# Text rows on 64 neighbouring partitions, transposed by one DMA instead of nine matrix products

## The chip, the cores and the metric

The kernel runs on one core of a Trainium2 chip. A core has a matrix engine (TensorE, "PE" in the profile; "PEld" is its loading of weights), VectorE ("DVE"), ScalarE ("ACT"), GpSimd ("POOL") and SyncE ("SP"), which work through their own instruction lists in order and wait for one another by semaphores, and 16 DMA engines that all queues share. SyncE, ScalarE and GpSimd can issue transfers, each on a queue of its own. The metric is device time in microseconds, lower is better.

## The reference

It is the joint attention block of a diffusion transformer, for two batches of 256 image tokens and 32 text tokens with 1152 features, one attention head over all features, in bfloat16. Image and text have weights of their own. Cut to what matters:

```python
mod_t = (_silu(c) @ wmod_txt).reshape(B, 6, 1, D)      # the same for the image
sht, sct, gat = mod_t[:, 0], mod_t[:, 1], mod_t[:, 2]
hi = _layernorm(x_img) * (1 + sci) + shi
ht = _layernorm(x_txt) * (1 + sct) + sht
qkvi = hi @ wqkv_img
qkvt = ht @ wqkv_txt
q, k, v = concat text and image rows of each
p = softmax(q @ k^T * D ** -0.5)
a = p @ v
out_i = x_img + gai * (a_img @ wo_img)
out_t = x_txt + gat * (a_txt @ wo_txt)
```

The change concerns `ht`: the text of both batches, 64 rows, is normalised, brought to features on partitions, scaled by `1 + sct` and shifted by `sht`. TensorE then needs it as the operand of the text's q, k and v.

## The kernel before

The 1152 features are KT = 9 tiles of 128. All instructions are issued in an order written out by hand (a manual schedule); each engine's list is the program text's order, so what a function issues stands on each engine's list where the function is called.

The weights, some 39 MB, come by SyncE's queue in the order of use, each matrix as `[128, 9, 1152]` into one of five buffers of a pool (`load_w`, line 73; some go to a home of their own). A load waits until its buffer's last reader is done. Each transfer also takes one of eight completion counters in turn and waits until the transfer that had it before has landed.

Work on the image comes first: normalising, transposing, scaling, then v, then q (`qk_img(w_q_i, 0, ...)`, line 519). Meanwhile VectorE forms the shift's part of v (`shift_products`, lines 468 to 474) in `sacc`. Then comes the stretch around the change, the image's k (line 589):

`qk_img` (line 503) walks over the nine output tiles j of k: the first three together, then one each. Every one is nine products of 128x512 summed in PSUM (`qkps`, line 512) and is evicted to `kT` by ScalarE or VectorE, as the list K_ENG says (j = 2, 4, 5, 6, 7 by ScalarE; 3 and 8 by VectorE). Before tile j it calls `hooks[j]`, so other work is put between the tiles:

- before j=3 `txt_norm`: VectorE takes statistics of x_t, ScalarE the square root, VectorE writes the normalised text back to x_t (line 179); ScalarE also loads the table of the exponential.
- before j=6 `row_strips`: TensorE forms the text's shift and scale as rows (`tsh`, `tsc`, line 402), evicted by ScalarE and VectorE, and the strip `svr`, evicted by ScalarE. GpSimd sends svr through device memory to `v_t` (lines 535 and 539).
- before j=7 `cols_and_transposes`: small products turn these rows into columns (`select_cols`, lines 418 and 420, `ctp`), evicted to `mod_t` by VectorE (line 423) and ScalarE (line 426). Then `txt_transposes` (line 559) multiplies each 128-column tile of x_t with every second column of the identity, which transposes it and picks the 64 text rows in one (line 565, into `tpt` in PSUM). VectorE multiplies with the scale out of PSUM (line 566), in two pieces, and adds the shift (line 569) in two. The result is hT_t, `[128, 9, 64]`.
- before j=8 `qk_txt(w_q_t, 0)`: 81 products of 128x64 with hT_t make the text's q (line 580).

After j=8, `qk_txt(w_k_t, 1)` makes the text's k, and scores, softmax, the text's v and the gates, attention, and the output products follow.

Before the change x_t has 128 partitions: the 64 text rows are loaded to every second one (line 444), and a memset by GpSimd (line 123) has put zeros into the others, so that normalising can run over all 128. The scale's weights `w_sc_t` come by two transfers.

Of the kernel before, what the change touches and what calls it, by code (L numbers as in the profile page):

```python
# [14 lines left out]
def kernel(  # L15
# [14 lines left out]
    nc = tc.nc  # L30
    bf = mybir.dt.bfloat16
    f32 = mybir.dt.float32
    PSUM = bass.MemoryType.PSUM

    B, NI, D = x_img.shape
    NT = x_txt.shape[1]
    P = 128
    KT = D // P
# [3 lines left out]
    NTT = B * NT  # L42
# [13 lines left out]
    work = ctx.enter_context(tc.tile_pool(name="work", bufs=2))  # L56
    small = ctx.enter_context(tc.tile_pool(name="small", bufs=4))
    ps_mm = ctx.enter_context(tc.tile_pool(name="ps_mm", bufs=7, space=PSUM))
# [6 lines left out]
    xt_flat = x_txt.rearrange("b n d -> (b n) d")  # L65
# [4 lines left out]
    def w_view(src):  # L70
        return src.rearrange("(kt p) n -> p kt n", p=P)

    def load_w(src, c0, ksplits=((0, KT),), home=None):
        t = wpool.tile([P, KT, D], bf, tag="w", name="t") if home is None else act.tile([P, KT, D], bf, tag=home, name="w_home")
        for (k0, k1) in ksplits:
            nc.sync.dma_start(t[:, k0:k1, :], w_view(src)[:, k0:k1, c0:c0 + D])
        return t
# [5 lines left out]
    x_t = act.tile([P, D], bf)  # L83
# [30 lines left out]
    K2 = ((0, 5), (5, KT))  # L114
# [4 lines left out]
    ident = const.tile([P, P], bf)  # L119
    make_identity(nc, ident[:])  # L120
    eps_t = const.tile([P, 1], f32)
    nc.vector.memset(eps_t[:], EPS)
    nc.gpsimd.memset(x_t[:], 0.0)
    wz = const.tile([P, VW], bf)
    nc.vector.memset(wz[:], 0.0)  # L125
    sT32 = const.tile([P, KT, 32], bf)
# [35 lines left out]
    def ln_stats(x_ap, np_, k0=0, k1=NCH, stats=None):  # L162
        if stats is None:
            stats = small.tile([P, NCH, 6], f32, tag="stats")
        for k in range(k0, k1):
            nc.vector.bn_stats(stats[0:np_, k, :], x_ap[:, k * CH:(k + 1) * CH])  # L166
        return stats

    def ln_std(stats, np_):
        mv = small.tile([P, 2], f32, tag="mv")  # L170
        nc.vector.bn_aggr(mv[0:np_, :], stats[0:np_, :, :])
        rstd = small.tile([P, 1], f32, tag="rstd")
        nc.scalar.activation(rstd[0:np_, :], mv[0:np_, 1:2], ACT.Sqrt, bias=eps_t[0:np_, :])
        return mv, rstd

    def ln_apply(x_ap, np_, out_ap, mv, rstd, c0=0, c1=D):
        if c0 == 0:
            nc.vector.reciprocal(rstd[0:np_, :], rstd[0:np_, :])
        nc.vector.tensor_scalar(out_ap[:, c0:c1], x_ap[:, c0:c1], mv[0:np_, 0:1], rstd[0:np_, :],
                                op0=ALU.subtract, op1=ALU.mult)  # L180
# [107 lines left out]
    lns = {}  # L288
# [59 lines left out]
    k0, k1 = KC[2]  # L348
# [14 lines left out]
    k0 = KC[3][0]  # L363
# [76 lines left out]

    w_k_i = load_w(wqkv_img, D, K3)
    w_sh_t = load_w(wmod_txt, 0)
    w_sc_t = load_w(wmod_txt, D, K2)
    nc.sync.dma_start(x_t[0:P:P // NTT, :], xt_flat[:, :])
    w_q_t = load_w(wqkv_txt, 0, K2)
    w_k_t = load_w(wqkv_txt, D, K2)
    w_ga_i = load_w(wmod_img, 2 * D, K2, home="V")
# [12 lines left out]
    def qk_evac(out_ap, in_ap, blk, eng=None):  # L460
        if blk == 0:
            nc.scalar.mul(out_ap, in_ap, SCALE)  # L462
        else:
            evac(out_ap, in_ap, eng)
# [15 lines left out]
    def shift_low(b):  # L480
        if b == 0:
            lo = work.tile([P, D], bf, tag="o", bufs=3, name="slo")
        else:
            lo_full = act.tile([P, D + 32], bf, name="slo_full")
            lo = lo_full[:, 0:D]
        sparts[1, b] = lo
        nc.vector.tensor_sub(lo[:, 0:D], saccs[b][:], sparts[0, b][:])
# [15 lines left out]
    def qk_img(wq, blk, jg, hooks):  # L503

        groups = [(0, jg)] + [(j, j + 1) for j in range(jg, KT)]
        for (j0, j1) in groups:
            if j0 in hooks:
                hooks[j0]()
            pss = [ps_mm.tile([P, B * NI], f32, tag="mm", name="qkps") for _ in range(j0, j1)]
            for kt in range(KT):  # L510
                for j in range(j0, j1):
                    nc.tensor.matmul(pss[j - j0][:], lhsT=wq[:, kt, j * P:(j + 1) * P], rhs=hT_i[:, kt, :],  # L512
                                     start=(kt == 0), stop=(kt == KT - 1))
            for j in range(j0, j1):
                qk_evac(qkTs[blk][:, j, :, 0:NI], pss[j - j0][:].rearrange("p (b n) -> p b n", b=B), blk, K_ENG[j])
# [27 lines left out]
    sv = sv_full[:, 0:KT * B].rearrange("p (k b) -> p k b", b=B)  # L543
    hT_t = act.tile([P, KT, NTT], bf)
    def txt_norm():
        lns = ln_std(ln_stats(x_t[:, :], P), P)
        shift_low(1)
        ln_apply(x_t[:, :], P, x_t[:, :], *lns)
        junk = small.tile([P, 1], f32, bufs=1)
        nc.scalar.activation(junk[:], eps_t[:], ACT.Exp)  # L550

    def all_cols():
        ctps = (ps_mm.tile([P, NCOL + B], f32, tag="mm", name="ctp"), ps_sm.tile([P, NCOL + B], f32, tag="sm", name="ctp"))
        for ctp, rows in zip(ctps, (strips["tsh"], strips["tsc"])):
            select_cols(rows, ctp)
        cols_out(mod_t[:, 1, :, :], ctps[1], 1.0)
        cols_copy(mod_t[:, 0, :, :], ctps[0])

    def txt_transposes():
        pick = ident[:].rearrange("p (t r) -> p r t", r=P // NTT)[:, 0, :]  # L560
        hv = hT_t[:].rearrange("p k (b t) -> p k b t", b=B)
        for k0, k1 in ((0, 5), (5, KT)):
            tpt = ps_mm.tile([P, 5, NTT], f32, tag="mm")
            for kt in range(k0, k1):
                nc.tensor.matmul(tpt[:, kt - k0, :], lhsT=x_t[:, kt * P:(kt + 1) * P], rhs=pick, start=True, stop=True)
            nc.vector.tensor_mul(hv[:, k0:k1], tpt[:, 0:k1 - k0, :].rearrange("p k (b t) -> p k b t", b=B),
                                 mod_t[:, 1, k0:k1, :].unsqueeze(3).to_broadcast([P, k1 - k0, B, NT]))
        for k0, k1 in ((0, 5), (5, KT)):
            nc.vector.tensor_add(hv[:, k0:k1], hv[:, k0:k1],
                                 mod_t[:, 0, k0:k1, :].unsqueeze(3).to_broadcast([P, k1 - k0, B, NT]))  # L570
# [3 lines left out]
    def qk_txt(wq, blk):  # L574
        for j0 in range(0, KT, FG):
            jn = min(FG, KT - j0)
            ps = ps_mm.tile([P, FG, NTT], f32, tag="mm")
            for j in range(j0, j0 + jn):
                for kt in range(KT):
                    nc.tensor.matmul(ps[:, j - j0, :], lhsT=wq[:, kt, j * P:(j + 1) * P], rhs=hT_t[:, kt, :],  # L580
                                     start=(kt == 0), stop=(kt == KT - 1))
            qk_evac(qkTs[blk][:, j0:j0 + jn, :, NI:NTOK],
                    ps[:, 0:jn, :].rearrange("p j (b n) -> p j b n", b=B), blk)

    def cols_and_transposes():
        all_cols()
        txt_transposes()

    qk_img(w_k_i, 1, 3, hooks={3: txt_norm, 6: row_strips, 7: cols_and_transposes, 8: lambda: qk_txt(w_q_t, 0)})
    qk_txt(w_k_t, 1)  # L590


# [330 lines left out]
```

## Time and profile before

| | |
|---|---|
| time, median of 3 runs | 114.87 us (114.75 to 115.28) |
| the profiled execution: its own time | 115.62 us |
| the profiled execution: span | 113.8 us |
| TensorE busy | 109.1 us (96%) |
| VectorE busy | 76.0 us (67%) |
| ScalarE busy | 37.4 us (33%) |
| GpSimd busy | 27.6 us (24%) |
| moved by DMA | 40.87 MB, mean 359 GB/s |
| mean granted TensorE clock | 0.998 |

The span runs from the first to the last instruction of one profiled execution; the device time has some two microseconds around it. An engine's busy share alone does not say whether it sets the end: for that there is the chain that ended last, followed back from the last instruction through whatever released each step. A row of the profile gives the engine, the line of the kernel, the operation, what it writes and reads, how often, and in brackets the idle time ahead of it with what ended it. In the rows in order of time the first number is the start in microseconds from the span's start and the second the length. In the rows of transfers the numbers are the size of each in KB and the microseconds from issue to landing.

### The profile page before, as it was taken

Reading aid. Unit: us, or ns where it says so; the run is one execution under the profiler, and the core shown is the slowest. Engines: PE = TensorE matmul, PEld = TensorE weight load, DVE = VectorE, ACT = ScalarE, POOL = GpSimd, SP = SyncE. Lnnn points to the kernel's source line nnn. Section 1 sums busy time; section 2 is a strip of 40 time slices with the busy share of each in tenths; the row PEclk is TensorE's granted clock in tenths of the full one; section 3 lists DMA queues with packets and bytes.
Section 4 is the critical chain, followed back from the end, with each engine's and each line's share of the span. In section 5 each row is a group of like instructions: output and inputs, shape, how many; then the busy total and the mean of one; then the engine's idle time right before and its main releaser. Section 6 shows DMA issues by size and latency. Waiting matters only on the chain.

```text
span 113.8 us, 2918 instructions
## 1 busy us (share of the span) xinstructions
PE 109.1 (96%) x1227; PEld 65.0 (57%) x1227; DVE 76.0 (67%) x151; ACT 37.4 (33%) x86; POOL 27.6 (24%) x60
## 2 busy tenths in 40 slices
PE   5999997999999999999999999999999999999990
PEld 1356663655644444444446659787687565667670
DVE  1699330756299999999999860236666802998771
ACT  4627500272290062640008934015546700001000
POOL 7000120640050000000000050601450460699300
PEclk9999999999999999999999999999999999999999
DMA  3999999999999999999999999999999999983052
GB/s 84 327 352 344 375 374 408 410 410 413 405 411 407 411 413 405 410 411 412 412 409 412 413 403 406 407 396 377 407 411 404 409 412 407 378 328 132 12 178 69
DMA packets 22839, 40.87 MB, mean 359 GB/s; under 512 B 1375, under 2 KB 6635, under 8 KB 22827
## 3 DMA queue, kind: packets, MB, share of 16 engines
q1 hardware_dynamic: 21547, 39.05, 89.8%
q10 hardware_dynamic: 672, 0.77, 2.2%
q0 software_dynamic: 608, 0.88, 2.1%
q8 instruction: 9, 0.15, 0.5%
q14 instruction: 3, 0.02, 0.1%
HBM read 39.36 MB, written 1.34 MB: 358 GB/s over the span
## 4 chain that ended last, share of the span: by engine, by line
PE 80%; SPq 8%; DMA 8%; issue 1%; DVE 0%
PE qkps L512 31%; PE ps L845 16%; DMA w_sc_i<-in_wmod_img_dram 8%; PE va L255 7%; SPq L98 6%; PE aps L753 5%; PE ps L580 4%; PE sps L613 4%; PE gps L402 3%; PE ops L863 2%; PE ps L688 2%; SPq L94 1%; PE van L267 1%; PE gps L818 1%; PE sps L626 1%; PE mps L217 1%
## 5 line engine op out<-in xcount | busy, mean ns | idle before, releaser
L512 PE MATMUL qkps<-hT_i,t 128*128 128x512 bf16 x162 | 35.6, 379 | 0.0
L512 PEld LDWEIGHTS <-t 128*128 128x128 bf16 x162 | 15.6, 98 | 18.6 <-issue 0.2
L474 DVE SCALAR_TENSOR_TENSOR sacc<-w_v_i,mod_img,sacc 128x1152 f32<-128x1152 bf16 x16 | 22.7, 1419 | 0.5
L255 PE MATMUL va<-w_v_i,hT_i 128*128 128x512 bf16 x72 | 17.5, 380 | 0.0
L845 PE MATMUL ps<-t,aT 128*128 128x384 bf16 x99 | 16.4, 326 | 0.0
L845 PEld LDWEIGHTS <-aT 128*128 128x128 bf16 x117 | 11.0, 98 | 6.9 <-issue 0.5
L851 DVE TENSOR_TENSOR tmp<-ps,gb 128x384 bf16<-128x384 f32 x11 | 6.1, 550 | 6.1 <-DMA gb<-mod_scratch 5.0
L829 POOL TENSOR_TENSOR w_og<-t,gb 128x384 bf16<-128x384 bf16 x9 | 8.7, 1004 | 4.6 <-DMA gb<-mod_scratch 4.6
L255 PEld LDWEIGHTS <-hT_i 128*128 128x128 bf16 x72 | 6.3, 98 | 5.6 <-ACT hT_i L201 0.4
L533 POOL TENSOR_SCALAR svn<-svr 128x128 bf16<-128x128 bf16 x1 | 0.3, 299 | 33.0 <-ACT svr L154 33.0
L140 PE MATMUL wps<-wz 128*128 128x512 bf16 x15 | 6.5, 613 | 1.2 <-DVE wz L125 1.2
L166 DVE BATCH_NORM_STATS2 stats<-x_i 128x6 f32<-128x384 bf16 x12 | 5.8, 541 | 2.5 <-DMA x_i<-in_x_img_dram 2.5
L462 ACT ACTIVATE qT<-qkps 128x512 bf16<-128x512 f32 x9 | 4.7, 602 | 7.1 <-PE qkps L512 7.1
L478 ACT CAST shi<-sacc 128x1152 bf16<-128x1152 f32 x2 | 2.3, 1152 | 13.0 <-DVE sacc L474 13.0
L240 POOL TENSOR_SCALAR hT_i<-hT_i,mod_img 128x128 bf16<-128x128 bf16 (+1 forms) x5 | 2.1, 435 | 15.8 <-DVE mod_img L225 15.8
L766 DVE TENSOR_SCALAR aT<-aps,sv 128x288 bf16<-128x288 f32 (+2 forms) x11 | 4.3, 456 | 2.0 <-PE aps L753 2.0
L235 DVE TENSOR_SCALAR hT_i<-hT_i,mod_img 128x256 bf16<-128x256 bf16 (+1 forms) x16 | 4.3, 328 | 1.7 <-ACT hT_i L212 1.5
L580 PEld LDWEIGHTS <-t 128*128 128x128 bf16 x162 | 5.0, 98 | 0.5
L154 DVE CAST kT<-qkps 128x512 bf16<-128x512 f32 x3 | 2.1, 686 | 4.7 <-PE qkps L512 4.7
L580 PE MATMUL ps<-hT_t,t 128*128 128x64 bf16 x162 | 5.1, 193 | 0.0
L852 DVE TENSOR_TENSOR o<-tmp,x_i 128x384 bf16<-128x384 bf16 x11 | 4.7, 426 | 0.4
L753 PE MATMUL aps<-pT,v_i 128*128 128x288 bf16 (+2 forms) x44 | 4.8, 265 | 0.0
(167 smaller groups left out, 146.2 us busy)
## 6 DMA issues: line engine op xcount, KB each, us to landing
t<-in_wqkv_img_dram SPq DMA_DIRECT2D x6, 864.0 KB, 13.0
t<-in_wmod_txt_dram SPq DMA_DIRECT2D x2, 2592.0 KB, 17.6
t<-in_wqkv_txt_dram SPq DMA_DIRECT2D x2, 1440.0 KB, 14.2
t<-in_wmod_img_dram SPq DMA_DIRECT2D x3, 864.0 KB, 12.3
t<-in_wqkv_txt_dram SPq DMA_DIRECT2D x3, 864.0 KB, 14.2
t<-in_wo_txt_dram SPq DMA_DIRECT2D x3, 864.0 KB, 15.5
t<-in_wqkv_txt_dram SPq DMA_DIRECT2D x2, 1152.0 KB, 15.0
w_v_i<-in_wqkv_img_dram SPq DMA_DIRECT2D x7, 288.0 KB, 7.1
```

The costliest lines, as they stand in the source:

```text
L98: nc.sync.dma_start(w_v_i[:, kt:kt + 1, :], w_view(wqkv_img)[:, kt:kt + 1, 2 * D:3 * D])
L140: nc.tensor.matmul(ps[:], lhsT=wz[:, 0:P], rhs=wz[:], start=True, stop=True)
L166: nc.vector.bn_stats(stats[0:np_, k, :], x_ap[:, k * CH:(k + 1) * CH])
L255: nc.tensor.matmul(ps[:], lhsT=hT_i[:, kt, i * P:(i + 1) * P], rhs=w_v_i[:, kt, half * VW:(half + 1) * VW], start=(kt == 0), stop=(kt == K ...
L462: nc.scalar.mul(out_ap, in_ap, SCALE)
L474: nc.vector.scalar_tensor_tensor(saccs[b][:], w_v_i[:, kt, :], ap, saccs[b][:], op0=ALU.mult, op1=ALU.add)
L512: nc.tensor.matmul(pss[j - j0][:], lhsT=wq[:, kt, j * P:(j + 1) * P], rhs=hT_i[:, kt, :], start=(kt == 0), stop=(kt == KT - 1))
L580: nc.tensor.matmul(ps[:, j - j0, :], lhsT=wq[:, kt, j * P:(j + 1) * P], rhs=hT_t[:, kt, :], start=(kt == 0), stop=(kt == KT - 1))
L753: nc.tensor.matmul(bank[:, off:off + c1 - c0], lhsT=lhsT, rhs=rhs, start=(first[id(bank)] == n), stop=(final[id(bank)] == n))
L829: nc.gpsimd.tensor_mul(w_og[:, dt, 0:CH], w_o_i[:, dt, NG0:D], gb[:, B - 1, NG0:D])
L845: nc.tensor.matmul(ps[:, 0:cw], lhsT=aT[:, dt, t0:t0 + P], rhs=rhs, start=(dt == DTS[0]), stop=(dt == DTS[-1]))
L851: nc.vector.tensor_mul(tmp[:, 0:cw], ps[:, 0:cw], gb[:, b, cs])
```

## The change

The text is loaded to partitions 0 to 63, and the memset of x_t goes. Normalising runs over 64 partitions. A hook before j=5 issues one transposing transfer on ScalarE's queue, from x_t to a new tile `xT_t` of `[128, 9, 64]` in SBUF; the tile takes a buffer of the pair that later holds the transposed probabilities (`pT`). The nine products with the picked identity and their two PSUM tiles go. The hook before j=7 still makes the columns and then scales and shifts, now reading xT_t. `w_sc_t` is loaded by one transfer instead of two.

```diff
--- before.py
+++ after.py
@@ -120,7 +120,6 @@
     make_identity(nc, ident[:])
     eps_t = const.tile([P, 1], f32)
     nc.vector.memset(eps_t[:], EPS)
-    nc.gpsimd.memset(x_t[:], 0.0)
     wz = const.tile([P, VW], bf)
     nc.vector.memset(wz[:], 0.0)
     sT32 = const.tile([P, KT, 32], bf)
@@ -440,8 +439,8 @@
 
     w_k_i = load_w(wqkv_img, D, K3)
     w_sh_t = load_w(wmod_txt, 0)
-    w_sc_t = load_w(wmod_txt, D, K2)
-    nc.sync.dma_start(x_t[0:P:P // NTT, :], xt_flat[:, :])
+    w_sc_t = load_w(wmod_txt, D)
+    nc.sync.dma_start(x_t[0:NTT, :], xt_flat[:, :])
     w_q_t = load_w(wqkv_txt, 0, K2)
     w_k_t = load_w(wqkv_txt, D, K2)
     w_ga_i = load_w(wmod_img, 2 * D, K2, home="V")
@@ -543,9 +542,9 @@
     sv = sv_full[:, 0:KT * B].rearrange("p (k b) -> p k b", b=B)
     hT_t = act.tile([P, KT, NTT], bf)
     def txt_norm():
-        lns = ln_std(ln_stats(x_t[:, :], P), P)
+        lns = ln_std(ln_stats(x_t[0:NTT, :], NTT), NTT)
         shift_low(1)
-        ln_apply(x_t[:, :], P, x_t[:, :], *lns)
+        ln_apply(x_t[0:NTT, :], NTT, x_t[0:NTT, :], *lns)
         junk = small.tile([P, 1], f32, bufs=1)
         nc.scalar.activation(junk[:], eps_t[:], ACT.Exp)
 
@@ -556,14 +555,16 @@
         cols_out(mod_t[:, 1, :, :], ctps[1], 1.0)
         cols_copy(mod_t[:, 0, :, :], ctps[0])
 
-    def txt_transposes():
-        pick = ident[:].rearrange("p (t r) -> p r t", r=P // NTT)[:, 0, :]
+    xT_t = work.tile([P, KT, NTT], bf, tag="pT", name="xT_t")
+
+    def txt_transposed():
+        nc.scalar.dma_start_transpose(xT_t[:], x_t[0:NTT, :])
+
+    def txt_modulated():
         hv = hT_t[:].rearrange("p k (b t) -> p k b t", b=B)
+        xv = xT_t[:].rearrange("p k (b t) -> p k b t", b=B)
         for k0, k1 in ((0, 5), (5, KT)):
-            tpt = ps_mm.tile([P, 5, NTT], f32, tag="mm")
-            for kt in range(k0, k1):
-                nc.tensor.matmul(tpt[:, kt - k0, :], lhsT=x_t[:, kt * P:(kt + 1) * P], rhs=pick, start=True, stop=True)
-            nc.vector.tensor_mul(hv[:, k0:k1], tpt[:, 0:k1 - k0, :].rearrange("p k (b t) -> p k b t", b=B),
+            nc.vector.tensor_mul(hv[:, k0:k1], xv[:, k0:k1],
                                  mod_t[:, 1, k0:k1, :].unsqueeze(3).to_broadcast([P, k1 - k0, B, NT]))
         for k0, k1 in ((0, 5), (5, KT)):
             nc.vector.tensor_add(hv[:, k0:k1], hv[:, k0:k1],
@@ -582,11 +583,11 @@
             qk_evac(qkTs[blk][:, j0:j0 + jn, :, NI:NTOK],
                     ps[:, 0:jn, :].rearrange("p j (b n) -> p j b n", b=B), blk)
 
-    def cols_and_transposes():
+    def cols_and_modulated():
         all_cols()
-        txt_transposes()
-
-    qk_img(w_k_i, 1, 3, hooks={3: txt_norm, 6: row_strips, 7: cols_and_transposes, 8: lambda: qk_txt(w_q_t, 0)})
+        txt_modulated()
+
+    qk_img(w_k_i, 1, 3, hooks={3: txt_norm, 5: txt_transposed, 6: row_strips, 7: cols_and_modulated, 8: lambda: qk_txt(w_q_t, 0)})
     qk_txt(w_k_t, 1)
 
 
```

## The prediction

> **What bounds the kernel now.** I read the busy shares first, then the chain that ended last, then the stretch of the change in order of time, then the landings of transfers.
>
> ```profile
> PE 109.1 (96%) x1227; PEld 65.0 (57%) x1227; DVE 76.0 (67%) x151; ACT 37.4 (33%) x86; POOL 27.6 (24%) x60
> DMA  3999999999999999999999999999999999983052
> ```
>
> TensorE is busy for 96% of the span, and the 16 DMA engines are full from the second slice almost to the end. Which of the two sets the end is told by the chain, in order of time (start, length, what):
>
> ```profile
> 63.96 2.05 PE qkps L512 x9
> 66.01 0.03 PE ctp L418 x2
> ...
> 66.14 0.29 PE tpt L565 x9
> 66.43 1.94 PE qkps L512 x9
> 68.37 2.36 PE ps L580 x81
> 70.73 1.94 PE qkps L512 x9
> 72.68 2.36 PE ps L580 x81
> ```
>
> From 19.60 to 111.04 us the chain is TensorE without one wait, so an instruction taken from it here shortens the kernel by its length, and a wait put into it lengthens it fully. The nine products that the change removes are the row with 0.29 us. The other engines in that stretch:
>
> ```profile
> 63.50 0.58 DVE L179 TENSOR_SCALAR x_t<-x_t,mv,rstd 128x1152 bf16<-128x1152 bf16 x1
> 63.93 1.05 ACT L154 CAST kT<-qkps 128x512 bf16<-128x512 f32 x2
> 64.87 0.49 ACT L154 CAST tsh<-gps 128x384 bf16<-128x384 f32 x1
> 66.18 0.18 DVE L423 TENSOR_SCALAR mod_txt<-ctp 128x18 f32<-128x18 f32 x1 [1.04 <-PE ctp L420]
> 66.46 0.82 DVE L566 TENSOR_TENSOR hT_t<-tpt,mod_txt 128x320 bf16<-128x320 f32 x2
> 67.20 0.82 DVE L569 TENSOR_TENSOR hT_t<-hT_t,mod_txt 128x320 bf16<-128x320 bf16 x2
> ```
>
> The reader is to see how late the text comes: it is normalised at 64.08, and hT_t, complete at 68.02, is what TensorE's row of 81 reads at 68.37. So 64.08 to 68.37 is all the room there is. What a transfer takes from issue to landing (KB each, us) is here:
>
> ```profile
> x_i<-in_x_img_dram ACTq DMA_DIRECT2D x2, 288.0 KB, 3.2
> gb<-mod_scratch POOLq DMA_DIRECT2D x2, 288.0 KB, 6.7
> v_t<-shift_scratch POOLq DMA_DIRECT2D x4, 32.0 KB, 5.4
> out_dram<-of ACTq DMA_DIRECT2D x3, 36.0 KB, 2.2
> shift_scratch<-svr POOLq DMA_DIRECT2D x2, 2.0 KB, 4.5
> ```
>
> The second x_i load of ScalarE's queue was issued at about 1.2 us, before the weight stream had filled, and the stores of `of` after it had ended; the other three rows ran beside the full stream.
>
> **The change part by part.**
>
> *Nine products leave TensorE* (L565, with their weight loads and two PSUM tiles): 0.29 us off the chain. Without them the products of j=7 begin at 66.14 and end at 68.08, and hT_t is needed there. This is all that the change can gain.
>
> *One transposing transfer joins ScalarE's queue.* In the order of the changed kernel it stands after the eviction of kT's strip j=4 and before that of j=5. Two evictions fill ScalarE's row from 63.93 to 64.98; the first takes 0.58, so the issue comes at about 64.45. Its data are ready (64.08), and the earlier transfer whose completion counter it takes over, the first third of w_k_i, was issued at 24.4 us and landed long before. How long it takes no row shows. By the nearest rows it lies between 2.9 us, the quicker x_i load of the same hardware queue, which had little beside it, and 7.2 us, the slower of the two gb loads, twice the bytes and beside the full stream. I go by the stretch, not by the queue, because at 64 us the DMA engines are full, as they were for v_t and gb. Between v_t (32 KB, 5.4) and gb (288 KB, 6.7), 144 KB gives 5.4 + 1.3 x 112/256 = 6.0 us by size. So it lands at 70.45.
>
> *VectorE's products then wait for that landing.* They read bfloat16 from SBUF in place of float32 from PSUM; the additions at L569, which read just so, take 0.82 for two, and so do the products of L566, so nothing changes in their length. From the first product to the last addition is 68.02 - 66.46 = 1.56 us. hT_t is complete at 70.45 + 1.56 = 72.0, with two handovers 72.15. Behind the waiting product on VectorE stand only the additions and kT's strip j=8, whose matmuls come after the wait; on TensorE the 81 products of qk_txt wait, and with them, the queue being in order, all the rest. Stall: 72.15 - 68.08 = 4.1 us; in general the landing time less 1.9. At 2.9 it is 1.0 and at 7.2 it is 5.3.
>
> *ScalarE is held while it issues.* Its rows for issues are 0.39 to 0.67 us, with the queue empty. After the issue it evicts j=5 and then tsh, which ended at 65.36 where TensorE took it at 66.01: 0.6 us of slack, so such an issue is hidden. SyncE's issues of a similar size take 2.7 us (x_t, 144 KB), since its ring is full; ScalarE's is empty. By 2.7 the select products would come 2.1 us late, but that time runs beside the flight of the transfer and adds nothing to a stall of 4.1. I take zero; the other end is a rival below. svr is late by the same, and behind it POOL's v_t loads, issued until 73.1 and landing 5.4 later; VectorE reads them at 83.00, so almost 5 us cover them.
>
> *POOL loses the memset of x_t* (1.05 us at 1.26). POOL's next work that anyone waits for, the copy of sT at 3.52, had waited 0.65 us for ScalarE even so: nothing gained. Normalising 64 partitions in place of 128 has the same elements per partition: VectorE's 545 ns per statistic and 0.58 for the result stay.
>
> *w_sc_t comes by one transfer instead of two.* The two were issued at 32.72 and 37.86 and took 19.1 and 16.9 to land, so the last byte was there at 54.8; SyncE moves the same bytes, and first use is the product row at 62.32. 7 us of cover. x_t, behind it on the queue, lands at 55.1 for a use at 60.44. One issue less and one more keep the turn of the eight completion counters; only the first part of w_o_i now waits for the transposition in place of w_q_t's second part. It waited 0.7 us for the products of L580 anyway (70.06 to 70.76), these come later with the stall, and its first use is behind 89.82: no cost.
>
> *144 KB more on the DMA engines* is 0.36 us of the stream at its 407 GB/s. Weights land before use from 19.6 us on (no DMA wait on the chain), so it costs nothing there.
>
> **Sum**: -0.29 + 4.1 = +3.8 us. Against the profiled execution's own 115.62 us (span 113.8) that is 119.4; that execution stood 0.75 above the median of 114.87, so against the median 118.7.
>
> **The rivals.**
>
> *The transfer is quick and the stall all but vanishes.* For this it must land like the stores of 36 KB on the same queue, 2.0 to 2.3 us: stall 0.1 to 0.4, which the 0.29 pays for, so 114.7 to 115.0, not slower. It decides at 2.2 us. For it: own queue, empty ring, SBUF to SBUF. Against it: those stores had 12 to 178 GB/s beside them in the last slices, here 407, and even 2 KB took 4.5 in this stretch. The Trainium skill's "DMA: Bandwidth & Descriptors" gives a fixed cost of about 2.0 us (section Anatomy of one DMA) and 261 GB/s for a transposing transfer of non-contiguous middle dimension (section Latency and other measured facts); that is an estimate of 2.6 us by that page and a sum of about +0.4, and the 4.5 us of 2 KB here disagrees with such a fixed cost under load. Chance 0.09.
>
> *ScalarE stays held until the transposition has landed.* Then tsh comes 6.0 us later, at 71.36, the selects end at 71.55, the products of j=7 at 73.5, and the stall is 73.5 - 68.08 = 5.4: +5.1, 120.0. It decides once the hold exceeds the landing time less about 1.3 us. For it: SyncE's rows show an issue that lasts for microseconds. Against it: those have a full ring. Chance 0.15.
>
> *The idle array loses its pace.* At the start, eleven of the 128x512 products of L140 take 4.65 us, 0.42 each; warm, nine such at L512 take 1.94, 0.22 each. So an array that comes from rest runs at half pace for up to some 6 us, which costs up to 3 us. In the kernel no rest from 19.6 us on tests this. The Trainium skill, "TensorE: Matmul & The Clock Gate" (Part 1), puts the loss at an idle window of 3.4 us, free-running; a stall of 4.1 would then seldom fill one. With the stall: 118.7 + 3 = 121.7 at most. Chance 0.12.
>
> **How the numbers follow.** Forecast (a stall of 1 to 5.5 us at full pace) 0.61, hidden 0.09, held 0.15, cold 0.12, other 0.03. Low end: landing after 2.9 gives +0.7, 115.6; I take 115.3, so that only the hidden case and a little lie under it. High end: the held case at 7.2 us is a stall of 6.6 and 121.2; with part of the cold price 122.5. About 0.5% (0.57 us) is what a measurement of this kernel can tell from no change. The largest gain, 0.29, is within it, so faster has 0.02, for what I have not seen; same 0.08; slower 0.90.
>
> **What would show it.** Right: a wait of VectorE's product of xT_t for the transfer, of 2 us or more, in place of the 1.04 for ctp; TensorE's L580 row beginning about 4 us after the j=7 row ended; the transposition's landing near 6 us; no tpt row. Held: ctp at L418 waits for tsh by several us and ScalarE's row has a gap. Cold: the 81 products after the stall at well over 29 ns apart. Wrong: a landing under 2.5 us, or a time that moves with no gap on TensorE around this place, so that a late weight or another queue would be the cause.

## The result, and the profile after

The changed kernel takes 123.91 us (median of 4 runs, 122.93 to 126.45) against 115.08 us (114.75 to 115.35) for the kernel before: a ratio of 1.074, 95% interval 1.068 to 1.080. It is slower, as forecast, but by 8.8 us and not by 3.8, and outside the stated range. One of the four, 126.45, was a slower execution at a lower granted clock (0.959 against 0.972), and the ratio leaves it out. The profiled execution took 122.93 us, the fastest of its kernel, with a span of 121.1.

From the page of the changed kernel: TensorE's busy time, the granted clock by slice, and the chain's shares.

```profile
PE 109.8 (91%) x1218; PEld 65.9 (54%) x1218; DVE 76.0 (63%) x151; ACT 37.4 (31%) x86; POOL 26.5 (22%) x59
...
PEclk9999999999999999999999965799999999999999
...
PE 55%; DVE 29%; DMA 11%; issue 1%; POOL 1%; ACTq 0%; DVEq 0%
```

TensorE still works for about 110 us, but over a longer span; the clock, full throughout before, falls to between 0.5 and 0.7 in three slices, 69.6 to 78.7 us; and the chain now runs through VectorE, behind whose sums of L473 (19%) the text is normalised, and through the transfer (8%).

The stretch of the change in order of time (start, length, what, and in brackets the idle time ahead and what ended it):

```profile
63.45 1.32 ACTq L561 DMA_TRANSPOSE xT_t<-x_t  x1
...
64.82 0.58 ACT L153 CAST kT<-qkps 128x512 bf16<-128x512 f32 x1 [0.96 <-DVE tsc L153]
...
65.84 0.20 PE L417 MATMUL ctp<-sel,tsh 128*128 128x8 bf16 x2 [0.45 <-ACT tsh L153]
...
66.00 2.10 PE L511 MATMUL qkps<-hT_i,t 128*128 128x512 bf16 x9
...
72.85 0.83 DVE L567 TENSOR_TENSOR hT_t<-xT_t,mod_txt 128x320 bf16<-128x320 bf16 x2 [6.50 <-DMA xT_t<-x_t]
...
74.23 3.86 PE L581 MATMUL ps<-hT_t,t 128*128 128x64 bf16 x81 [6.12 <-DVE hT_t L570]
...
77.92 2.11 PE L511 MATMUL qkps<-hT_i,t 128*128 128x512 bf16 x9
```

The reader is to see the transposition issued at 63.45, VectorE's product waiting 6.5 us for it, and TensorE resting 6.12 us ahead of the text's q. Then its 81 products take 3.86 us. Before, in the same view, they took 2.52:

```profile
68.21 2.52 PE L580 MATMUL ps<-hT_t,t 128*128 128x64 bf16 x81
```

The landing, and the packets of ScalarE's queue (q10) and the weight queue (q1) between 62 and 76 us (packets, MB, share of 16 engines):

```profile
q1 hardware_dynamic: 2341, 5.23, 98.6%
q10 hardware_dynamic: 608, 0.15, 6.7%
...
xT_t<-x_t ACTq DMA_TRANSPOSE x1, 9.3
```

Set from the start of the products of j=6, which both kernels reach with the same work done (63.90 us before, 63.27 after), the time goes like this:

| from the start of j=6 to the start of | before, us | after, us | later by |
|---|---|---|---|
| the select products (ctp) | 1.95 | 2.57 | 0.62 |
| j=7 | 2.37 | 2.73 | 0.36 |
| the text's q (L580, L581) | 4.31 | 10.96 | 6.65 |
| j=8 | 6.67 | 14.65 | 7.98 |
| the scores | 11.00 | 18.99 | 7.99 |
| the last VectorE row | 47.16 | 55.16 | 8.00 |

All 8.0 us are lost between the issue and the end of the text's q, 6.65 by its later start and 1.33 in slower products (3.69 from the text's q to j=8, against 2.36). The spans differ by 7.3 because this execution of the changed kernel had reached j=6 0.63 us sooner: its products with the last part of w_sc_i began at 18.99 us, and those of the kernel before at 19.60, after a wait of 0.69 us for that load.

### The profile page after: what moved, and what is told of

Read it like the earlier page. It is cut to its first block, busy times and chain, and to the rows that moved or that the text cites. A ratio compares the mean times of both kernels' runs of the same rounds, so it can differ in the third digit from the quotient of the medians.

```text
span 121.1 us, 2899 instructions
## 1 busy us (share of the span) xinstructions
PE 109.8 (91%) x1218; PEld 65.9 (54%) x1218; DVE 76.0 (63%) x151; ACT 37.4 (31%) x86; POOL 26.5 (22%) x59
## 4 chain that ended last, share of the span: by engine, by line
PE 55%; DVE 29%; DMA 11%; issue 1%; POOL 1%; ACTq 0%; DVEq 0%
DVE sacc L473 19%; PE ps L846 15%; PE va L254 12%; DMA xT_t<-x_t 8%; PE ps L581 5%; PE aps L754 4%; PE sps L614 4%; DMA x_i<-in_x_img_dram 4%; DVE stats L165 2%; PE ops L864 2%; PE van L266 2%; PE ps L689 2%; PE qkps L511 2%; PE mps L216 1%; DVE sacc L471 1%; DVE slo L486 1%
## 5 line engine op out<-in xcount | busy, mean ns | idle before, releaser
L511 PEld LDWEIGHTS <-t 128*128 128x128 bf16 x162 | 15.6, 98 | 18.6 <-issue 0.2
L473 DVE SCALAR_TENSOR_TENSOR sacc<-w_v_i,mod_img,sacc 128x1152 f32<-128x1152 bf16 x16 | 22.7, 1418 | 0.5
L581 PE MATMUL ps<-hT_t,t 128*128 128x64 bf16 x162 | 6.4, 209 | 6.1 <-DVE hT_t L570 6.1
L581 PEld LDWEIGHTS <-t 128*128 128x128 bf16 x162 | 6.3, 109 | 6.8 <-issue 6.6
L139 PE MATMUL wps<-wz 128*128 128x512 bf16 x15 | 5.6, 537 | 1.2 <-DVE wz L124 1.2
L477 ACT CAST shi<-sacc 128x1152 bf16<-128x1152 f32 x2 | 2.3, 1152 | 13.0 <-DVE sacc L473 13.0
L567 DVE TENSOR_TENSOR hT_t<-xT_t,mod_txt 128x320 bf16<-128x320 bf16 (+1 forms) x2 | 0.8, 454 | 6.5 <-DMA xT_t<-x_t 6.5
## 6 DMA issues: line engine op xcount, KB each, us to landing
t<-in_wqkv_img_dram SPq DMA_DIRECT2D x6, 864.0 KB, 13.2
```

The lines of the kernel that those rows point to most:

```text
L139: nc.tensor.matmul(ps[:], lhsT=wz[:, 0:P], rhs=wz[:], start=True, stop=True)
L473: nc.vector.scalar_tensor_tensor(saccs[b][:], w_v_i[:, kt, :], ap, saccs[b][:], op0=ALU.mult, op1=ALU.add)
```

## The experiments

My theory after this result: the flight of the transposition is the loss, it lasts 9.3 us because of the number of its pieces, and TensorE's rest costs its pace besides. Rivals: that other parts of the change cost (the layout, the one transfer for w_sc_t), that the flight is long for another reason (the load, the turning itself), and that the 81 products are slow for another reason than the rest.

**The change without its transfer.**

```diff
-    def txt_transposed():
-        nc.scalar.dma_start_transpose(xT_t[:], x_t[0:NTT, :])
...
+            tpt = ps_mm.tile([P, 5, NTT], f32, tag="mm")
+            for kt in range(k0, k1):
+                nc.tensor.matmul(tpt[:, kt - k0, :], lhsT=x_t[0:NTT, kt * P:(kt + 1) * P],
+                                 rhs=ident[0:NTT, 0:NTT], start=True, stop=True)
```

> The changed kernel without the transposing transfer: text on 64 neighbouring partitions, no memset, w_sc_t by one transfer, but nine products with the 64x64 corner of the identity transpose it as before. Theory (the transfer's flight is the whole loss): within 0.5% of the kernel before, 114.5 to 115.6 us, TensorE without a gap between j=7 and L580. Rival (the layout, the one transfer for w_sc_t or the turn of the counters costs too): 1 us or more above before.

Measured: 115.79 us against 115.08, ratio 1.0051 (1.0025 to 1.0078). So without the transfer 8.1 of the 8.8 us are gone, and TensorE has no gap between j=7 and the text's q. The remaining 0.5% is small, but its interval lies wholly above 1; that part of my theory did not hold, and two runs below look for it.

**The transfer without readers.** The same kernel, with the transposition issued as in the change, its tile read by nobody.

> As the kernel that transposes on TensorE, with the transposing transfer still issued at the same place on ScalarE's queue, into a tile that nobody reads. It shows the flight without the stall, and what the issue and the transfer cost by themselves. Theory: landing again 8 to 11 us after the issue, ScalarE held about 1.3 us, the selects up to 0.6 us late, so 115.1 to 116.0 us. Rival (the transfer's presence disturbs the weight stream or SyncE's counters, and that is a part of the loss): 117 us or more. Rival (the flight is long only because TensorE rests or what follows waits): landing under 6 us.

Measured: 117.08 us, ratio 1.0157 (1.0093 to 1.0220). In the profiled execution the image's first loads came some 3 us late, so only durations within it are read. The issue and the landing of xT_t in it:

```profile
L561 ACTq DMA_TRANSPOSE xT_t<-x_t x1: 1331/1331/1331, 66.5 to 66.5; - x1
...
DMA to landing us min/median/max: 9.3/9.3/9.3
```

With nobody waiting, the flight lasts 9.3 us again: it is a property of the transfer at this place and not of the stall. By the two ratios the transfer itself costs some 1.2 us over the kernel without it (1.0157 less 1.0051), from few runs that spread over 1.1 us. That is above what I expected. The median just meets the first rival's 117 us, two of the runs stay under it at 116.5, and a part of that rival holds. In the profile TensorE waits 0.48 us for tsh at the selects, since ScalarE is held 1.33 us, and 0.51 us later in the text's k, for which no releaser is named. And the 16 DMA engines moved 349 and 319 GB/s in the four microseconds from 70 us on, against some 400; in the changed kernel, too, it was 278 and 384 from 68 to 72 us (the windows below), where the kernel before moved 412 and 409. So the transfer takes more from the stream than its own bytes.

**The rest filled with idle products.**

```diff
+    def filled_qk_txt():
+        ps = ps_mm.tile([P, VW], f32, tag="mm", name="wps")
+        for _ in range(27):
+            nc.tensor.matmul(ps[:], lhsT=wz[:, 0:P], rhs=wz[:], start=True, stop=True)
+        qk_txt(w_q_t, 0)
...
-8: lambda: qk_txt(w_q_t, 0)
+8: filled_qk_txt
```

> The changed kernel with 27 idle 128x512 products of zeros (27 x 0.216 = 5.8 us at full pace) put into TensorE's list ahead of the text's q, where it rests about 6.1 us; their result is read by nobody. Theory (the rest lowers the array's pace, and the 81 products after it pay 1.5 us): the 81 products take 2.4 us instead of 3.86 and the time falls by 1.0 to 1.6 us against the changed kernel, to about 122.4. Rival (the 81 products are slow for another reason, hT_t arriving in pieces or the engines' contention): no change or slower by up to 0.5 us.

Measured: 123.46 us, ratio to before 1.0708 (1.0632 to 1.0783). The changed kernel by windows of 2 us (length, then busy time and instructions of TensorE, its weight loads, VectorE, ScalarE, GpSimd; then granted clock, DMA share, GB/s):

```profile
68.00:70.00 2.00, 0.11 (x1) 0.00 (x0) 0.00 (x0) 0.58 (x1) 0.00 (x0) 1.00 1.12 278
70.00:72.00 2.00, 0.00 (x0) 0.00 (x0) 0.00 (x0) 0.00 (x0) 0.00 (x0) 0.60 1.09 384
72.00:74.00 2.00, 0.00 (x0) 0.00 (x0) 1.15 (x3) 0.00 (x0) 1.42 (x3) 0.50 1.04 402
74.00:76.00 2.00, 1.77 (x34) 1.80 (x35) 0.42 (x2) 0.00 (x0) 0.59 (x2) 0.50 1.06 418
76.00:78.00 2.00, 2.00 (x52) 2.00 (x50) 0.00 (x0) 0.49 (x1) 0.00 (x0) 0.70 1.05 400
```

and the filled kernel's text q in order of time:

```profile
68.05 5.99 PE L593 MATMUL wps<-wz 128*128 128x512 bf16 x27
74.36 2.62 PE L581 MATMUL ps<-hT_t,t 128*128 128x64 bf16 x81 [0.32 <-DVE hT_t L570]
```

In finer windows the clock is 1.00 until 70.25 us and 0.50 from 70.50, some 2.3 us after the last product's end at 68.1, and it is back at 1.00 from 77.25, 3.0 us after work has resumed at 74.23. Filled, the clock stays at 1.00 and the 81 products take 2.62 instead of 3.86, so the rest is what slows them. All four runs of the filled kernel have a mean clock of 0.997 or more, against 0.972 at best in the changed one. The gain of 1.2 us there does not show as clearly in the time: the profiled executions differ by 0.8 us in their spans (120.3 against 121.1), the medians by 0.3 (123.46 against 123.77, by the runs that the ratios take), with intervals that overlap. The saving of 1.0 us or more that I expected of the time was not measured.

**The same transfer, 29 us earlier.** The text is loaded ahead of w_sh_i, its statistics are taken in VectorE's pause at 28.4 us, and the transposition is issued at 34.6.

```diff
+    nc.sync.dma_start(x_t[0:NTT, :], xt_flat[:, :])
     w_sh_i = load_w(wmod_img, 0, K3)
...
     v_narrow(3, 0, KT)
+    tstats = ln_stats(x_t[0:NTT, :], NTT)
...
     shr = rows_for_cols(w_sh_i, "shr")
+    tlns = ln_std(tstats, NTT)
...
     evac(v_i[:, :, NM:D], vacc["n"][:])
+    ln_apply(x_t[0:NTT, :], NTT, x_t[0:NTT, :], *tlns)
+    nc.scalar.dma_start_transpose(xT_t[:], x_t[0:NTT, :])
```

> The changed kernel with the text loaded ahead of the image's shift weights, its statistics in VectorE's pause at 29 us, the normalised text ready at about 35 us and the same transposing transfer issued there on ScalarE, some 30 us before hT_t is made. Theory (the flight is long, and it costs only because it starts late): no wait for xT_t, the nine products saved, 114.0 to 115.2 us. Rival (a transposing transfer costs the streams beside it wherever it is): 116 us or more, with a gap where a weight comes late.

Measured: 115.72 us, ratio 1.0052 (1.0031 to 1.0073). It lands after 8.7 us, no one waits for it, and the nine products are saved. So lateness is what made it cost 8 us. But it is not faster than before, and 0.5 us above the upper end of what I expected. Where the saving goes is seen in the text's v, in order of time:

```profile
80.43 1.47 PE L688 MATMUL ps<-t,hT_t 128*32 128x512 bf16 x24
82.15 0.83 PE L688 MATMUL ps<-t,hT_t 128*32 128x512 bf16 x12 [0.25 <-DMA t<-in_wqkv_txt_dram]
```

TensorE comes sooner and waits for the last third of w_v_t. In the kernel before, that third was issued at 67.93 and landed 13.7 later, at 81.6, with its first reader due at about 82.1: half a microsecond of slack, so the stream of weights is almost as late as TensorE. Counted from the start of j=6, the early kernel's profiled execution is 0.26 us ahead at j=7 and 0.2 us behind at the end (47.39 against 47.16). The other 0.4 us between the medians is not located.

**How long a transfer of 144 KB flies, by pieces.** Five kernels, all with the transposition done on TensorE and an unread transfer of the text. Each was run once, so their landings, not their times, are compared. The first copies plainly, in rows of 2304 bytes.

```diff
-        nc.scalar.dma_start_transpose(xT_t[:], x_t[0:NTT, :])
+        nc.scalar.dma_start(xT_t[:].rearrange("p k t -> p (k t)")[NTT:P, 0:D], x_t[0:NTT, :])
```

> As the kernel with the unread transfer, but the same 144 KB at the same place on ScalarE's queue are copied plainly, without transposing, into an unread tile, in 64 rows of 2304 bytes (4 for each DMA engine). Theory 'turns' (the transposition goes in 576 pieces of 256 bytes, 36 for each of 16 engines, and each waits for the weight stream's packet on its engine): landing 3.5 to 5.5 us after the issue. Rival 'load' (any transfer beside the full stream takes as long): 8 to 10 us.

```profile
xT_t<-x_t ACTq DMA_DIRECT2D x1, 144.0 KB, 6.4
```

It landed after 6.4 us, between the two expectations and nearer to that of the turns.

The second copies plainly in 576 pieces:

```diff
+        nc.scalar.dma_start(xT_t[NTT:P, :, 0:P], x_t[0:NTT, :].rearrange("q (k j) -> q k j", k=KT))
```

> The same plain copy cut into 576 pieces of 256 bytes by leaving gaps in the unread tile: as many pieces for each engine as the transposition has, and nothing transposed. Theory 'turns': landing 7 to 9.5 us after the issue, close to the transposition's 9.3. Rival 'transposing' (turning the data, not the number of pieces, takes the time): 3.5 to 5.5 us, as the copy in long rows.

```profile
xT_t<-x_t ACTq DMA_DIRECT2D x1, 144.0 KB, 9.3
```

The same 9.3 us as the transposition, with nothing transposed: the turning costs no time that shows beside the pieces. The third transposes five of the nine column tiles:

```diff
+        nc.scalar.dma_start_transpose(xT_t[:, 0:5, :], x_t[0:NTT, 0:5 * P])
```

> As the kernel with the unread transposition, but of the first five of nine column tiles only: 320 pieces, 20 for each engine. Theory 'turns': a fixed part of 3 to 4 us and 0.15 to 0.17 us for each of an engine's pieces, so 6.0 to 7.0 us to landing. Rival (a fixed cost that the size does not move): 8.5 to 9.3 us.

```profile
xT_t<-x_t ACTq DMA_TRANSPOSE x1, 7.7
```

Again between the two expectations. The fixed part is larger than I had put it, 6.0 us and not 3 to 4, and each piece costs less: 0.09 us.

The fourth issues the full transposition when the weights are almost over, behind the eviction of the text's gate at 103.5 us.

> The kernel that transposes on TensorE, with the full unread transposition issued on ScalarE's queue behind the eviction of the text's gate, at about 103 us, when the weight stream has ended. Theory 'turns': no stream to wait for, so 3 to 4.5 us to landing, with an issue still near 1.3 us. Rival 'transposing': 8 to 9.3 us as beside the stream.

```profile
L823 ACTq DMA_TRANSPOSE xT_t<-x_t x1: 1935/1935/1935, 103.5 to 103.5; - x1
...
DMA to landing us min/median/max: 3.1/3.1/3.1
```

Three times as quick with the stream almost over (196 GB/s in the first microsecond from 103 us, 78 in the next); the issue held ScalarE longer (1.94 us). With a line through 4 pieces (6.4) and 36 (9.3), (9.3 - 6.4)/32 = 0.0906 us for each piece and 6.04 fixed, the fifth kernel was forecast, with 1152 pieces of 128 bytes:

```diff
+        nc.scalar.dma_start(xT_t[NTT:P, :, 0:64], x_t[0:NTT, :].rearrange("q (k j) -> q k j", k=2 * KT))
```

> The unread plain copy of 144 KB cut into 1152 pieces of 128 bytes, 72 for each engine. Four pieces landed after 6.4 us, 36 after 9.3, and 20 (the half transposition) after 7.7, which is 6.04 + 0.0906 us for each piece. Theory 'turns': 6.04 + 72 x 0.0906 = 12.6 us, 11.5 to 13.5. Rival (the pieces' number stops to matter, or the bytes decide): 9 to 10 us.

```profile
xT_t<-x_t ACTq DMA_DIRECT2D x1, 144.0 KB, 13.2
```

| pieces for each engine | what | landing, us | line, us |
|---|---|---|---|
| 4 | plain, 2304 B | 6.4 | (6.4) |
| 20 | half transposition | 7.7 | 7.85 |
| 36 | plain, 256 B | 9.3 | (9.3) |
| 36 | transposition | 9.3 | 9.3 |
| 72 | plain, 128 B | 13.2 | 12.6 |
| 36 | transposition, weights almost over | 3.1 | |

Bytes do not set the time (the same 144 KB in 6.4, 9.3 and 13.2 us), pieces do. And 0.09 us is what a weight packet takes: in the kernel before, the weight queue moved 5.16 MB in 2308 packets between 63 and 76 us, 2236 bytes each, and the engines 407 GB/s or 25.4 each, so 88 ns. So the times fit a DMA engine that serves the two queues in turn, as many pieces of ours as packets of the weights. That is inferred from this agreement, which is rough: between the rows of the table a piece costs 0.08, then 0.10, then 0.11 us, and our own packets need some 25 ns each besides (6.7% of 14 us on 16 engines for 608). Whether a turn is one piece or several, the slope does not tell; the queues' order on an engine was not seen directly, and the fixed 6 us are not explained. The Trainium skill, "DMA: Bandwidth & Descriptors" (section Queues, rings and completion order), says that an engine goes round the queues that have work packet by packet, and these runs fit that: ScalarE's queue shows 608 packets in the changed kernel's lines above, 576 and 2 more for each engine.

**What the small rest is.** The kernel without the transfer was 0.5% slow. Two candidates, split. First the 64 neighbouring partitions (and the missing memset) with w_sc_t by two transfers again:

```diff
-    w_sc_t = load_w(wmod_txt, D)
+    w_sc_t = load_w(wmod_txt, D, K2)
```

> The kernel on 64 neighbouring partitions that transposes on TensorE, with w_sc_t again by two transfers: of the change only the layout of x_t (and the missing memset) is left. In the kernel with both, the stream fell to about 350 GB/s for some 2.5 us just before x_t landed, and the last third of w_v_t came late. Theory (loading x_t to 64 neighbouring partitions slows the stream): 0.3 to 0.7 us above before, with that dip between 52 and 56 us. Rival (the one long transfer for w_sc_t does it): no dip, within 0.2 us of before.

Measured: 115.88 against 114.88 us, ratio 1.0112 (1.0054 to 1.0171). Its windows, ahead of the landing of x_t:

```profile
52.00:54.00 2.00, 2.00 (x11) 0.88 (x9) 1.93 (x3) 0.00 (x0) 0.00 (x0) 1.00 1.06 325
54.00:56.00 2.00, 2.00 (x11) 0.89 (x10) 1.96 (x2) 0.00 (x0) 0.00 (x0) 1.00 1.04 372
```

Then the kernel before with only w_sc_t by one transfer:

> The kernel before with one edit: w_sc_t by one transfer instead of two. Theory (layout): no dip in the stream, within 0.2 us of before. Rival (the long transfer): a dip ahead of x_t's landing and 0.3 to 0.7 us more.

Measured: 115.19 us, ratio 1.0023 (0.9981 to 1.0065), and the same windows:

```profile
52.00:54.00 2.00, 2.00 (x11) 0.94 (x10) 1.97 (x2) 0.00 (x0) 0.00 (x0) 1.00 1.03 407
54.00:56.00 2.00, 2.00 (x11) 0.91 (x10) 1.97 (x2) 0.00 (x0) 0.00 (x0) 1.00 1.04 411
```

Its median is 0.3 us above before, a little more than the 0.2 that I expected, but the interval holds 1. The dip comes with the layout of x_t and not with the long transfer. All ten kernels that load x_t onto 64 neighbouring partitions at this place have it (290 to 372 GB/s in the two windows), and the early kernel, which loads it sooner, does not have it here but at 20 to 22 us (340 GB/s, against 411 before). In the split kernel (411 - 325 + 411 - 372) GB/s x 2 us is 0.25 MB, about 0.6 us of the stream. That this is what makes the time longer is shown only in part. In five of the seven kernels that have the layout and a transfer nobody waits for (early, plain in long rows, plain in 256 bytes, half, quiet) TensorE waits 0.25 to 0.85 us for the last third of w_v_t. In the profiled execution of the split kernel it doesn't, and that one's span (114.0 us) is hardly above before's. The layout costs 0.5 to 1.1% by the ratios of the two kernels without a transfer, 0.25 to 1.7% with their intervals; its path is left open.

No version tried beats the kernel before. The early transposition comes nearest among those that keep the transfer, and what it saves on TensorE the weights take back.

## Why the prediction was wrong

The mechanism, TensorE's wait for the landing, was right; the size was not, and two costs that the sum put at nothing were there.

- *The bound.* TensorE's chain without a wait, so that a stall counts fully: right. The 6.65 us by which the text's q began late are found whole at the end.
- *Nine products leave TensorE, 0.29 us.* Right: 0.26 from the selects to j=7.
- *The landing, 6.0 us.* This is the step that failed. I worked it out from the bytes, between 32 KB at 5.4 and 288 KB at 6.7, and bounded it by 7.2, the slower gb load, as if a transfer of twice the bytes had to be slower. It measured 9.3. The sum had no term for pieces: 576 of 256 bytes, 36 for each engine at 0.09 us, 3.3 us, beside a fixed part of 6.0 that the interpolation by chance hit. With 9.3 in its place my own rule, landing less 1.9 less 0.29, gives 7.1. The issue came 0.4 us sooner after j=6 began than I had it (0.18 against 0.55), because it did not wait for the end of the eviction ahead of it (63.29 to 63.85). That and the next point give 6.5, against the measured 6.65.
- *VectorE after the landing, 1.56 us and handovers, 1.7 in all.* Nearly right: 1.5 from the landing at 72.75 to the text's q at 74.23. TensorE began before the second addition had ended (74.42).
- *ScalarE's hold, taken as nothing.* Off, without weight in the sum. The issue took 1.32 us instead of 0.39 to 0.67, beyond the slack of 0.6 that I had counted, and the selects were 0.62 us late; as the prediction said for this case, that ran beside the flight. The prediction laid SyncE's long issues to a full ring. The load of x_t fits that, with 0.58 us for its issue at 14.0 us in the early kernel and 2.69 at 43.2 in the kernel before; but ScalarE's queue was empty here, and the issue was long all the same. The rival in which ScalarE stays held until the landing did not occur.
- *The idle array loses its pace*, chance 0.12, up to 3 us: this rival came true together with the forecast, at 1.33 us. I had set it apart because a stall of 4.1 us seemed too short for it. The Trainium skill's "TensorE: Matmul & The Clock Gate" (Part 1) puts the loss at an idle window of 3.4 us, and the granted clock does not agree with a full window of rest: it was at 0.50 from 70.50 us on, some 2.3 us after the last product. So even the stall that I forecast would have been long enough by this run, and the price belonged into the sum. 6.65 + 1.33 is the table's 8.0.
- *The quick transfer*, chance 0.09: did not occur here. Its landing, 2 to 2.3 us, was not far off for a quiet machine (3.1), which this stretch is not. The fixed 2.0 us that the prediction quoted from the Trainium skill is given there for transfers that GpSimd issues, and the sum did not use it.
- *Costs put at nothing.* One transfer for w_sc_t: right (ratio 1.0023, with 1 in its interval). The layout of 64 partitions: wrong by some 0.5 to 1%; I had looked at VectorE's time alone and not at how the load lands. "Weights land before use, so it costs nothing": no wait for a weight is seen in the changed kernel, but unread the transfer cost some 1.2 us, and the slack at w_v_t is half a microsecond, which I had not looked for; the early version used it up.

The upper end failed with the landing: it held 7.2 us and part of the cold price, and nothing for pieces.

## What to carry to other kernels

In this kernel a transfer that shared the DMA engines with a full stream was priced by its pieces, not its bytes. As an estimate elsewhere, count the contiguous runs for each engine, multiply by the time of the stream's packet, and add the fixed time that the neighbours of the stretch show. The transposing transfer here went in 576 pieces of 256 bytes and took 9.3 us, so it belonged where its result is needed 10 us later or more, not between two steps that are 4 us apart. And where TensorE sets the end and may rest for some microseconds, add the loss of pace to the stall instead of counting it as another case: here the clock fell 2.3 us into the rest.

## What the runs showed of the hardware

- The transposing transfer took just as long as a plain copy in as many pieces: 9.3 us both. Its flight hardly changed between four profiled executions beside the stream (9.3, 9.3, 9.3 and 8.7 us), and was 3.1 us with the stream almost over.
- The issue of a transposing transfer held ScalarE for 1.30 to 1.33 us beside the stream and 1.94 in the quiet, against 0.55 to 0.71 for the plain copies; half the columns made it no shorter (1.30).
- A load of 144 KB onto 64 neighbouring partitions lowered the whole stream from 411 to 325 and 372 GB/s in two windows ahead of its landing, and to 290 to 372 in all ten kernels that loaded it there; the same rows on every second partition did not.
- The clock granted to TensorE went from 1.00 to 0.50 some 2.3 us into a rest of 6 us and was back at 1.00 some 3.0 us after work resumed. In the kernel that filled the rest it stayed at 1.00.
